# Attention and a gated FFN on one core: the first block's FFN in later slots, and four more score tiles taken transposed

## The chip, the cores and the metric

The kernel runs on one core of a Trainium2 chip. Its engines are TensorE (PE in the profile, its weight loads PEld), VectorE (DVE), ScalarE (ACT), GpSimd (POOL), and SyncE (SP), which here only issues DMAs. The metric is the time of one execution on the device in microseconds (us). The kernel before takes 1466.86 us (median of three runs, 1466.7 to 1467.34).

## The reference

For each of 4 batches, with S = 3136 rows, 256 columns and keys of width 64:

```python
scores = (1 / S) * z @ z.T              # S x S: keys and queries are the same z
x = u * (np.maximum(scores, 0) ** 2 @ v)  # attention without a softmax, gated by u
h = np.maximum(x @ w_in, 0)             # 256 -> 1024
conv = conv_w[0] * h[t - 1] + conv_w[1] * h[t] + conv_w[2] * h[t + 1]   # along the rows
out = (h * sigmoid(conv)) @ w_out       # 1024 -> 256
```

The score matrix of a batch is symmetric: the tile of keys j under queries q is the transpose of the tile of keys q under queries j.

## The kernel before

**Tiles.** The queries of a batch are cut into 6 blocks of 512 and a remainder of 64, the keys into 25 tiles of 128 (the last holds 64 rows, twice). All products are made of float32 values that are split into a high and a low part, so that one logical matmul is two or three on TensorE: 2 for a score tile (lines 409 and 410), 6 for a tile's share of the attention (line 535: three for each half of the 256 columns), 6 for one FFN input tile of 128 columns (`ffn_in`, lines 705 to 708), 6 for one FFN output share (`ffn_out`, lines 780 to 782, three for each half).

**Slots.** The whole program is written out by hand as 600 slots, one for each key tile of each of the 24 blocks; every engine executes its instructions in the order in which the slots name them. In slot k TensorE does the attention of tile k (`attend`) and the scores of tile k + 4 (`scores`); the other engines prepare tiles k + 2 and k + 3. A score tile s in PSUM becomes t = relu(s) on ScalarE (line 489, three buffers `t`), is squared on VectorE (line 504; on ScalarE for the tiles in `SQ`), is cast to the high part `ah` on ScalarE (line 513) and subtracted to the low part `al` on VectorE (line 171). `al` is the last reader of the score bank. There are two banks `s`; for tiles below `K_O` the odd ones use `ph` (block 0) or `o0`/`o1` instead, so that four are in turn.

**Transposed tiles.** Where the symmetry allows, a block doesn't score a tile but takes what an earlier block has: there GpSimd copies relu(s) as two halves of 16 bits to a buffer `pl` (`part`, line 439, three buffers), SP writes it to DRAM (`spill`, line 452), and ten slots before its use SP reads it back with a transposing DMA (`fetch`). ScalarE then squares it, and for even slots squares it a second time into `ah`; VectorE only makes `al` (in odd slots also the cast). `Q0` says how many query blocks of batch 0 score the four tiles of block 0's columns for themselves; from block `Q0` on these come transposed, and block 0 writes them out (`entries`, `own`, `part`).

**FFN.** When a block's attention is done, `gate_x` takes it from the two `av` banks and multiplies by u in the first slot of the next block; `split_x` makes the two parts `xh` and `xl`. Then the eight FFN tiles f follow in slots given by `FS`, counted from the block's first slot: `ffn_in` into one of two banks `ph`, a relu and a first tap on ScalarE, two convolution steps on VectorE (line 749), a sigmoid, a gate product (line 763, four slots after `ffn_in`, the last use of the bank), the split, and `ffn_out` ten and eleven slots after `ffn_in`, into `o0` and `o1`. `evac` and `store` write the block's result 12 and 14 slots after the last tile's slot. The banks `ph` serve two other things once a block: the ring score (line 377, freed by a relu on ScalarE, line 383) three slots before the block begins, and from block 2 on an early score of the last key tile (line 546, freed by a copy, line 551), in most blocks in slot 6.

**Weights.** The weights come as 64-bit floats and are turned into two float32 parts on the chip, in 16 pieces (8 of `w_in`, 8 of `w_out`, in the order of need) that begin in the slots `WS` and are loaded four slots earlier. A piece takes four instructions on VectorE (lines 316, 320, 328, 333), two and a cast on ScalarE (lines 325, 326, 174), a product and a subtraction on GpSimd (lines 338 and 171). Its intermediate values lie in a PSUM bank (`wp` in the trace) for pieces that begin before slot `W_P` and those in `W_B`, in SBUF (`wr`) for the others.

**What else block 0 holds.** In the first 25 slots GpSimd and ScalarE also split the keys (`zl`, `zh`) and the values (`vv`).

Of the kernel before, what the change touches and what calls it, by code (L numbers as in the profile page):

```python
# [30 lines left out]
DG = [1, 8, 15, 22]  # L31


K_O = 35
Q0 = 3
C0 = [0, 1, 2, 3, 16, 17, 22, 23, 4, 5, 18, 19, 8, 9, 20, 21, 6, 7, 10, 11, 14, 15, 12, 13, 24]

FS = [2, 5, 8, 11, 15, 18, 21, 24]  # L40
RELU, TAP, ST1, ST2, SIG, GATE, GHI, OUT0, OUT1 = 1, 2, 2, 3, 4, 4, 5, 10, 11
EVAC = 12
UL = 18
XS = 1

C_GATE, C_ST1, C_ST2, C_G, C_SIG, C_HI = 0, 2, 2, 2, 1, 3
C_RELU, C_TAP, C_XS, C_EV, C_V = 3, 1, 3, 3, 5
# [2 lines left out]
WARM = 7  # L50
VO = 4
Z1 = -3
WS = [2, 6, 8, 12, 16, 19, 21, 25, 27, 33, 36, 38, 40, 41, 46, 52]
WST = [0, 1, 1, 2, 3]
W_E = ["GGGGGGGGGGGGGGGG", "AAAAAAAAAAAAAAAA"]
W_C = 7
W_A = [9, 14]
W_B = [6, 7]
SQ = [26, 46]
W_P = 22  # L60

# [18 lines left out]
def kernel(  # L80
# [21 lines left out]
    NJ = (S + P - 1) // P  # L102
# [5 lines left out]
    FC = DFF // P  # L108
# [12 lines left out]
    def own(b, q):  # L121
        return CB if b == 0 and q < Q0 else 0

# [273 lines left out]
    def scores(k):  # L397
# [3 lines left out]

        if k < K_O and k % 2:
            tag, n = ("ph", 2) if k < NJ else (f"o{k // 2 % 2}", 1)
# [23 lines left out]
    def part(k):  # L427
# [3 lines left out]
        if x is not None and x < CB - 1:  # L431
            src = rl[k][:, (x + 1) * P : (x + 2) * P if x else NB]
        elif x is None and not (tr or r < (Q0 if b == q == 0 else q + 1) or (r == QB and q >= RB)):
            src = rl[k]
# [384 lines left out]
    V, A, G = nc.vector, nc.scalar, nc.gpsimd  # L819
# [4 lines left out]
    PRE, MID, VEC, POST, PE0, PE1 = range(6)  # L824

    def at(slot, cls, fn, *args):
        ev[slot][cls].append((fn, args))
# [3 lines left out]
    for q in zs[2:]:  # L831
        s = min(C0.index(j) for j in range(q * CB, min(q * CB + CB, NJ))) - LA - 3
# [11 lines left out]
    for b in range(1, B):  # L844
        k0 = (b * QB - 1) * NJ
        for q in range(QB + 1):
            s = k0 - (QB - 2 - q) * NJ + (12 if q % 2 == 0 else 4)
            if q == QB - 2:
                s = k0 + 6
            elif q == QB - 1:  # L850
                s = k0 + NJ + 6
            elif q == QB:
                s = k0 + 9
            if b == 1 and q < 2:
                s = (Q0 - QB) * NJ + NJ + k0 + 4 + 8 * q
            at(s - 4, POST, load_z, b, q)
            at(s, POST, prep_z, q)
        last = {j: i for i, (j, _) in enumerate(ent[b - 1][QB - 1])}
        for j in range(0, NJ, 2):
            s = k0 + max(last[j] + 2, last.get(j + 1, 0) + 2, V0 + V1 * j // NJ)  # L860
            if j == NJ - 1:
                s = k0 + V0 - 2
# [5 lines left out]
    for blk in range(1, NBLK):  # L868
        s = blk * NJ + E3
# [4 lines left out]
    for blk in range(PK, NBLK):  # L874
        s = blk * NJ + (R_E if blk % QB == RB else E24[blk % QB])
# [6 lines left out]
    for b in range(B):  # L882
# [9 lines left out]
        for i in range(n + 1):  # L892
            s = k5 + (R_J + 2 * i + R_L * (i == n - 1) // 2 if i < n else R_D + 1) + 1
# [14 lines left out]
    def prep_w_at(n, what, f, i, s):  # L908
        if not wps and W_P:
            wps["w"] = ps.tile([P, 2, D], F32, tag="o1", name="wp")  # L910
        bank = wps["w"] if s < W_P else None
        if i in W_B and not n:
            bank = ps.tile([P, 512], F32, tag="ph", name="wp", bufs=2).rearrange("p (a n) -> p a n", a=2)
        prep_w(n, what, f, *(E[x[i]] for x in W_E), bank, nc.gpsimd if i in W_A else None)

    need = [(NJ + FS[f], "in", f) for f in range(FC)] + [(NJ + FS[f] + OUT0, "out", f) for f in range(FC)]
    for i, (_, what, f) in enumerate(sorted(need)):
        s = WS[i]
        at(s - 4, POST, load_w, what, f)
# [2 lines left out]
    for n in range(4):  # L922
        at(W_C + n, POST, prep_conv, n)
    for blk in range(NBLK):
        at(blk * NJ + UL, POST, load_u, blk)

    def before_end(slot, *args):
        if slot < NS:
            at(slot, *args)

    for blk in range(NBLK - 1):
        k0 = (blk + 1) * NJ
        at(k0, C_GATE, gate_x, blk, G)
        at(k0 + XS, C_XS, split_x, blk, (V, G))
        for f in range(FC):
            s = k0 + FS[f]
            if s == NS - 1:
                break
            at(s, POST, ffn_halo, blk, f)
            at(s, PE1, ffn_in, blk, f)  # L940
            at(s + RELU, C_RELU, ffn_relu, blk, f)
            at(s + RELU, C_RELU, ffn_keep, blk, f)
            at(s + TAP, C_TAP, ffn_tap, blk, f)
            at(s + ST1, C_ST1, ffn_conv, blk, f, 1)
            at(s + ST2, C_ST2, ffn_conv, blk, f, 2)
            before_end(s + SIG, C_SIG, ffn_sig, blk, f)
            before_end(s + GATE, C_G, ffn_gate, blk, f, G)
            before_end(s + GHI, C_HI, ffn_hi, blk, f, A)
            before_end(s + GHI, PE1, ffn_lo, blk, f, G)
            before_end(s + OUT0, PE0, ffn_out, blk, f, 0)  # L950
            before_end(s + OUT1, PE0, ffn_out, blk, f, 1)
        if blk < NBLK - 2:
            at(s + EVAC, C_EV, evac, blk)
            at(s + EVAC + 2, POST, store, blk)
# [97 lines left out]
    def run(fns):  # L1052
        for fn, args in fns:
            fn(*args)

    with tc.manual_schedule():
# [15 lines left out]
        for k in range(-LA, NS):  # L1072
            e = ev[k]
            run(e[PRE])
            early = k + LT < K_O
            if early and 0 <= k + LT:
# [81 lines left out]
```

## Time and profile before

| | |
|---|---|
| median of three runs | 1466.86 us |
| profiled execution | 1467.12 us |
| its span, first to last instruction | 1465.3 us |
| busy PE, PEld | 1451.6 us, 1260.7 us |
| busy DVE, ACT, POOL | 1143.4, 1178.5, 864.0 us |
| matmuls | 6781 |
| granted TensorE clock, mean | 1.000 |

A busy time is the time in which at least one instruction of the engine is recorded. Records of neighbouring instructions overlap, those of matmuls most: one of 512 columns is recorded with 0.38 us and the next begins 0.22 us later. So the share of busy time says little of how full TensorE is, and counts of matmuls in a stretch say more. Block 0 runs from 8.4 to 55 us, block 1 to about 120 us, block 2 to 180 us.

### The profile page before, as it was taken

What the parts mean: (1) busy time and instruction counts of PE and PEld (TensorE: products, weight loads), DVE (VectorE), ACT (ScalarE), POOL (GpSimd) and SP (SyncE); (2) the same over time, 40 slices, a digit from 0 to 9 for tenths busy, and PEclk for the clock granted to TensorE, in tenths of its full rate; (3) what the DMA queues carried; (4) which work ended last, traced back from release to release, by engine and by line L of the source; (5) the groups of instructions that cost most, each with busy time, mean ns of one, the idle gap of its engine ahead of it and who ended that gap; (6) DMA issues with size and microseconds to landing.
All of it is one profiled execution on the core that took longest, in us unless ns stands there. A gap on an engine that the chain in (4) does not pass through costs nothing.

```text
span 1465.3 us, 22715 instructions
## 1 busy us (share of the span) xinstructions
PE 1451.6 (99%) x6781; PEld 1260.7 (86%) x6781; DVE 1143.4 (78%) x1776; ACT 1178.5 (80%) x2246; POOL 864.0 (59%) x1218
## 2 busy tenths in 40 slices
PE   9999999999999999999999999999999999999998
PEld 7778888888888888888888888888888888888887
DVE  8998777768787777767777877876778777787677
ACT  8878887878877877878888788787887777878767
POOL 7875656447866654545776654554586654554433
PEclk9999999999999999999999999999999999999999
DMA  6544666865445556678444555586644446567621
GB/s 198 164 132 104 153 142 156 169 150 138 147 134 142 135 132 157 138 149 178 133 149 132 138 140 134 140 172 138 157 149 137 132 122 150 129 132 168 133 63 37
DMA packets 432380, 205.24 MB, mean 140 GB/s; under 512 B 330753, under 2 KB 411905, under 8 KB 432257
## 3 DMA queue, kind: packets, MB, share of 16 engines
q1 hardware_dynamic: 431584, 203.40, 56.9%
q8 instruction: 53, 0.87, 0.3%
q14 instruction: 71, 0.57, 0.1%
q10 hardware_dynamic: 672, 0.40, 0.1%
HBM read 36.59 MB, written 86.90 MB: 84 GB/s over the span
## 4 chain that ended last, share of the span: by engine, by line
PE 87%; POOL 4%; ACT 3%; DVE 3%; issue 2%; DMA 0%; SPq 0%; ACTq 0%; POOLq 0%; DVEq 0%
PE av L535 46%; PE ph L708 5%; PE o L780 5%; PE o L782 5%; PE ph L705 5%; PE o L781 5%; PE ph L706 5%; PE s L409 4%; PE s L410 4%; PE av L617 1%; DVE ph L749 1%; POOL vv L171 1%; POOL pl L439 1%; ACT ph L744 1%; DVE al L171 1%
## 5 line engine op out<-in xcount | busy, mean ns | idle before, releaser
L535 PE MATMUL av<-ah,vv 128*128 128x512 f32 x2400 | 708.7, 379 | 1.4 <-ACT ah L513 0.7
L171 DVE TENSOR_TENSOR al<-s,ah 128x512 fp32r<-128x512 f32 x576 | 397.5, 690 | 225.4 <-PE av L535 116.8
L535 PEld LDWEIGHTS av<-ah,vv 128*128 128x128 f32 x2400 | 449.5, 189 | 64.9 <-ACT ah L513 1.1
L535 PE MATMUL av<-al,vv 128*128 128x512 f32 x1152 | 437.0, 379 | 0.4
L171 POOL TENSOR_TENSOR gl<-hb,gh 128x512 fp32r<-128x512 f32 x192 | 245.3, 1277 | 157.1 <-ACT gh L174 149.3
L749 DVE SCALAR_TENSOR_TENSOR ph<-hb,cw,ph 128x512 f32<-128x512 f32 x384 | 286.8, 747 | 9.4 <-ACT ph L744 9.0
L439 POOL COPY pl<-t 128x1024 uint16<-128x1024 uint16 (+1 forms) x257 | 260.9, 1017 | 2.2 <-DMA dq<-pl 1.1
L535 PEld LDWEIGHTS av<-al,vv 128*128 128x128 f32 x1152 | 217.7, 189 | 32.6 <-DVE al L171 1.8
L504 DVE TENSOR_TENSOR s<-s,t 128x512 f32<-128x512 f32 x275 | 191.8, 697 | 61.5 <-ACT t L489 60.8
L489 ACT ACTIVATE t<-s 128x512 f32<-128x512 f32 x277 | 166.1, 599 | 64.1 <-PE s L410 60.0
L513 ACT CAST ah<-s 128x512 fp32r<-128x512 f32 x277 | 163.3, 590 | 59.8 <-DVE s L504 59.5
L756 ACT ACTIVATE ph<-ph 128x512 f32<-128x512 f32 (+1 forms) x200 | 115.4, 577 | 78.1 <-DVE ph L749 74.7
L739 POOL COPY halo<-hb 128x2 f32<-128x2 f32 x160 | 31.1, 194 | 240.6 <-ACT hb L734 232.2
L484 ACT ACTIVATE s<-tp 128x512 f32<-128x512 f32 x278 | 165.3, 596 | 4.9 <-DMA tp<-dd 3.0
L705 PE MATMUL ph<-xh,wih 128*128 128x512 f32 x384 | 145.8, 380 | 1.1 <-DVE hb L763 1.1
L780 PE MATMUL o<-gh,wol 128*128 128x512 f32 x384 | 145.9, 380 | 0.0
L782 PE MATMUL o<-gl,woh 128*128 128x512 f32 x384 | 145.5, 379 | 0.0
L706 PE MATMUL ph<-xh,wil 128*128 128x512 f32 x384 | 145.5, 379 | 0.0
L781 PE MATMUL o<-gh,woh 128*128 128x512 f32 x384 | 145.5, 379 | 0.0
L744 ACT ACTIVATE ph<-hb,cw 128x512 f32<-128x512 f32 x192 | 133.7, 696 | 6.2 <-POOL halo L739 0.4
L763 DVE TENSOR_TENSOR hb<-ph,hb 128x512 f32<-128x512 f32 x192 | 131.8, 686 | 5.1 <-ACT ph L756 0.7
L734 ACT ACTIVATE hb<-ph 128x512 f32<-128x512 f32 x192 | 114.2, 595 | 17.7 <-PE ph L708 16.3
(138 smaller groups left out, 2091.3 us busy)
## 6 DMA issues: line engine op xcount, KB each, us to landing
dq<-pl SPq DMA_DIRECT2D x232, 256.0 KB, 2.7
st<-in_v_dram SPq DMA_DIRECT2D x48, 256.0 KB, 3.1
ut<-in_u_dram SPq DMA_DIRECT2D x24, 512.0 KB, 4.1
out_dram<-ob SPq DMA_DIRECT2D x19, 512.0 KB, 3.8
st<-in_z_dram SPq DMA_DIRECT2D x24, 256.0 KB, 3.2
sh<-sc SPq DMA_DIRECT2D x44, 128.0 KB, 2.4
dd<-pl SPq DMA_DIRECT2D x69, 64.0 KB, 2.2
dd<-pl SPq DMA_DIRECT2D x23, 192.0 KB, 2.4
```

What stands on the lines that cost most here:

```text
L171: eng.tensor_tensor(out=out, in0=a, in1=b.bitcast(F32), op=ALU.subtract)
L439: nc.gpsimd.tensor_copy(pl[k], src.bitcast(U16).rearrange("p (n h) -> p h n", h=2))
L484: nc.scalar.activation(sc[k][:, :NB], tp[k], AF.Square, scale=SC1**-0.5)
L489: nc.scalar.activation(rl[k], sc[k][:, :NB], AF.Relu, scale=SC1)
L504: nc.vector.tensor_tensor(out=s, in0=s, in1=rl[k], op=ALU.mult)
L535: nc.tensor.matmul(o, lhsT=w[:, j, d], rhs=pairs(r), start=first and i == 0, stop=last and i == len(ops) - 1)
L705: nc.tensor.matmul(o, lhsT=wih[:, dc, w], rhs=pairs(xh[blk][:, dc]), start=(dc == 0), stop=False)
L706: nc.tensor.matmul(o, lhsT=wil[:, dc, w], rhs=pairs(xh[blk][:, dc]), start=False, stop=False)
L749: nc.vector.scalar_tensor_tensor(out=c, in0=hb[blk, f][:, k : e + k], scalar=cw[:, f, k : k + 1], in1=c, op0=ALU.mult, op1=ALU.add,)
L780: nc.tensor.matmul(o, lhsT=wol[:, f, d], rhs=pairs(h), start=(f == 0), stop=False)
L781: nc.tensor.matmul(o, lhsT=woh[:, f, d], rhs=pairs(h), start=False, stop=False)
L782: nc.tensor.matmul(o, lhsT=woh[:, f, d], rhs=pairs(l), start=False, stop=(f == FC - 1))
```

## The change

Block 0's FFN begins in slot 32 and no longer in slot 27: a block's FFN lags by `max(0, 5 - block)` slots, and while it does its eight tiles come every third slot (`FSL`), so that the lag is gone with block 5. `split_x` moves with it; `gate_x` doesn't. The loads of u for blocks 2 and 3 are two slots and one slot later. The pieces of the weights begin in later slots, the last in 57 instead of 52, and piece 8 too uses a PSUM bank. `K_O` goes from 35 to 40: five more slots in which odd score tiles use the banks `o0` and `o1` and a relu is issued ahead of the cast. `Q0` goes from 3 to 2: block 2 takes its tiles of keys 0 to 3 transposed, and block 0 writes out tiles 8 to 11, which it didn't before.

```diff
-K_O = 35
-Q0 = 3
+K_O = 40
+Q0 = 2
 FS = [2, 5, 8, 11, 15, 18, 21, 24]
+FSL = [2, 5, 8, 11, 14, 17, 20, 23]
+LAG = 5
-WS = [2, 6, 8, 12, 16, 19, 21, 25, 27, 33, 36, 38, 40, 41, 46, 52]
+WS = [2, 6, 10, 13, 17, 20, 24, 28, 32, 36, 39, 43, 46, 49, 53, 57]
-W_B = [6, 7]
+W_B = [6, 7, 8]
...
-    need = [(NJ + FS[f], "in", f) for f in range(FC)] + [(NJ + FS[f] + OUT0, "out", f) for f in range(FC)]
+    def lag(blk):
+        return max(0, LAG - blk)
+
+    def ffn_slots(blk):
+        x = lag(blk)
+        return [(blk + 1) * NJ + x + s for s in (FSL if x else FS)]
+
+    need = [(s + o, w, f) for w, o in (("in", 0), ("out", OUT0)) for f, s in enumerate(ffn_slots(0))]
...
-        at(blk * NJ + UL, POST, load_u, blk)
+        at(blk * NJ + max(UL, lag(blk - 2) + 15 if blk > 1 else 0), POST, load_u, blk)
...
-        at(k0 + XS, C_XS, split_x, blk, (V, G))
-        for f in range(FC):
-            s = k0 + FS[f]
+        at(k0 + XS + lag(blk), C_XS, split_x, blk, (V, G))
+        for f, s in enumerate(ffn_slots(blk)):
```

## Rows read from the trace of the kernel before

**Rows 1.** The page, part 4: the chain that ended last, by engine.

```profile
PE 87%; POOL 4%; ACT 3%; DVE 3%; issue 2%; DMA 0%; SPq 0%; ACTq 0%; POOLq 0%; DVEq 0%
```

**Rows 2.** Busy time by stretch: length, each engine's busy time (instructions), clock, DMA share, GB/s.

```profile
40.00:60.00 20.00, 19.04 (x84) 14.94 (x83) 19.20 (x38) 17.39 (x39) 16.39 (x22) 1.00 0.61 180
60.00:80.00 20.00, 19.28 (x86) 15.52 (x85) 18.88 (x33) 17.16 (x36) 13.50 (x21) 1.00 0.39 109
80.00:100.00 20.00, 17.94 (x81) 14.50 (x81) 19.33 (x34) 16.50 (x35) 14.91 (x20) 1.00 0.45 130
100.00:120.00 20.00, 19.54 (x90) 16.40 (x89) 18.19 (x29) 16.46 (x34) 17.04 (x25) 1.00 0.50 147
...
140.00:200.00 60.00, 60.00 (x283) 52.62 (x282) 46.90 (x71) 48.61 (x91) 35.44 (x49) 1.00 0.65 146
```

**Rows 3.** Waits of PEld, 8 to 120 us: us in total, times, longest.

```profile
PEld s L409 <- DVE al L171: 5.3, 9, 2.0
```

**Rows 4.** Waits of ACT, 8 to 120 us.

```profile
ACT t L489 <- POOL pl L439: 1.3, 2, 1.1
```

**Rows 5.** DMA issues, 0 to 60 us: count, size, median us to landing.

```profile
dq<-pl SPq DMA_DIRECT2D x12, 256.0 KB, 3.2
```

**Rows 6.** POOL groups, 28.8 to 51.02 us: count, busy us, mean ns, idle before them.

```profile
L439 POOL COPY pl<-t 128x1024 uint16<-128x1024 uint16 x7 | 7.2, 1041 | 0.0
...
L338 POOL TENSOR_TENSOR wr<-wr 128x256 f32<-128x256 f32 x4 | 2.9, 735 | 1.1 <-DVE wr L333 1.1
L171 POOL TENSOR_TENSOR wil<-wr,wih 128x256 fp32r<-128x256 f32 x4 | 2.9, 733 | 0.0
```

**Rows 7.** DVE groups by form, 8 to 120 us.

```profile
L749 DVE SCALAR_TENSOR_TENSOR ph<-hb,cw,ph 128x512 f32<-128x512 f32 x14 | 10.4, 745 | 0.0
L328 DVE SCALAR_TENSOR_TENSOR wr<-wr 128x256 uint32<-128x256 uint32 x7 | 4.9, 697 | 0.0
...
L316 DVE TENSOR_SCALAR wr<-wr 128x256 uint32<-128x256 uint32 x7 | 4.0, 573 | 0.0
...
L328 DVE SCALAR_TENSOR_TENSOR wr<-wr,wp 128x256 uint32<-128x256 uint32 x8 | 3.7, 466 | 0.0
L320 DVE TENSOR_SCALAR wr<-wr 128x256 uint32<-128x256 uint32 x7 | 3.6, 520 | 0.0
L333 DVE SCALAR_TENSOR_TENSOR wr<-wr 128x256 f32<-128x256 uint32 x5 | 3.0, 605 | 0.0
```

**Rows 8.** DVE in order of time, 92 to 99 us: start, us, line.

```profile
92.77 0.68 DVE L171 TENSOR_TENSOR al<-s,ah 128x512 fp32r<-128x512 f32 x1
93.37 0.69 DVE L504 TENSOR_TENSOR s<-s,t 128x512 f32<-128x512 f32 x1
93.97 0.68 DVE L763 TENSOR_TENSOR hb<-ph,hb 128x512 f32<-128x512 f32 x1
```

**Rows 9.** All engines in order of time, 48 to 56 us: the end of block 0.

```profile
49.96 1.04 POOL L439 COPY pl<-t 128x1024 uint16<-128x1024 uint16 x1
...
51.29 0.59 ACT L489 ACTIVATE t<-s 128x512 f32<-128x512 f32 x1
...
54.14 0.44 ACT L174 CAST woh<-wr 128x256 fp32r<-128x256 f32 x1
...
55.15 1.24 PE L535 MATMUL av<-ah,vv 128*128 128x512 f32 x3 [0.60 <-ACT x L667]
```

**Rows 10.** The same, 110 to 116 and 136 to 138 us: users of `ph`.

```profile
110.08 0.38 PE L705 MATMUL ph<-xh,wih 128*128 128x512 f32 x1
...
112.44 0.68 DVE L763 TENSOR_TENSOR hb<-ph,hb 128x512 f32<-128x512 f32 x1
...
113.97 0.60 PE L535 MATMUL av<-ah,vv 128*128 128x512 f32 x2
...
114.84 0.40 ACT L383 ACTIVATE dg<-ph 128x256 f32<-128x256 f32 x1
...
137.16 0.59 ACT L551 COPY sc<-ph 128x512 f32<-128x512 f32 x1
137.33 0.59 PE L535 MATMUL av<-ah,vv 128*128 128x512 f32 x2
```

## The prediction, before the kernel was run

> **What bounds the kernel now.** I read the page first: of the chain that ended last TensorE holds 87% and no other engine over 4% [rows 1]; the span is 1465.3 us. Over most of the run TensorE sets the time, and only a change in its work, or a stall of TensorE, moves the end. Next the busy times by stretch [rows 2]. The busy share is of little use (a matmul's recorded time overlaps the next), the count of matmuls is: 283 in the 60 us from 140 on, so a matmul of full width takes 0.212 us and 20 us hold 94.3. From 40 to 120 us they hold 84, 86, 81 and 90. The shortfall is 10.3 matmuls (2.2 us) from 40 to 60, and 8.3, 13.3 and 4.3 (25.9, or 5.5 us) from 60 to 120. From 140 on it holds its rate. So about 8 us can be had from stalls, all in block 0's last slots and in the two stages after. The reader is to see that VectorE is busy 18.2 to 19.3 us of every 20 there, GpSimd 13.5 to 17.0. Third the waits: TensorE waits nine times (5.3 us in its weight loads) for VectorE's `al`, the last reader of a score bank [rows 3]; ScalarE waits for GpSimd's copy of a score tile to `pl` in 1.3 us [rows 4]. The granted clock is 1.00 in all these stretches.
>
> I use slots: one key tile of one query block, 25 a block. A slot without FFN is 8 matmuls, 1.7 us.
>
> **The change, part by part.**
>
> *Eight matmuls go.* In block 2 four tiles are no longer scored but come transposed: 4 x 2 x 0.212 = 1.7 us. Block 2 lies in the stretch at full rate [rows 2], so I take all of it; bounded by 1.7 and, if that stretch waits for something else then, 0. Their VectorE squares (0.69 us each [rows 8]) go too; ScalarE squares twice where it had a relu and a copy. Four transposes of 256 KB join SP's queue, ten slots ahead. Four transposed tiles of block 2 were there before, in the stretch from 140 on, and lost nothing [rows 2]; the DMA share there is 0.65. So I put the new four at nothing; were that cover gone, a late tile would hold TensorE for about one landing, 3.2 us [rows 5].
>
> *Four GpSimd copies, and four spills, come into block 0.* With `Q0` 2 the tiles 8 to 11 are written out as well: parts at positions 4 to 7, 10 to 15 and 18 to 23, where 12, 13, 18 and 19 had none. GpSimd is full there: from 28.8 to 51.0 us its only gap is 1.1 us, before a weight piece's product on line 338 [rows 6]. To the copy for tile 23, which ends at 51.0 us [rows 9], the new order adds 4 x 1.04 = 4.2 us, loses one weight step (0.73 us) through the later pieces, and can use the gap: 4.2 - 0.7 - 1.1 = 2.4. Who waits: there are three `t` buffers, so ScalarE's relu three tiles on waits for the copy, and behind that relu, in order, stand the casts to `ah` and block 0's scaled evacuation on line 667, for which TensorE waits at 55.15 us [rows 9]. The relu began 0.3 us after the copy's end, and a weight cast in between (0.44 us) moves later: 2.4 - 0.7 = 1.7 us lost. Bounds: 0, if the order of the buffers leaves slack, and 2.4 + 1.1 = 3.5, if the gap stays. I take 1.7, since GpSimd has no other gap. The spills queue on SP behind GpSimd's copies; with three `pl` buffers and a landing of 3.2 us [rows 5] against copies 1.7 us apart or more they just fit.
>
> *The FFN begins five slots later and the pieces are spread.* This takes work away from VectorE where it was late. Its instructions begin 0.09 us before their forerunner's record ends (they start at 92.77, 93.37 and 93.97, with records of 0.68 to 0.69) [rows 8]. Slots 36 to 42 before (79 to 100 us): 6 squares and 7 `al` of 0.69 (9.0 us), 4 convolution steps of 0.75 (3.0), 2 gate products of 0.68 (1.4), 4 weight pieces (begun at 36, 38, 40 and 41) of 0.57 + 0.52 + 0.70 + 0.61 = 2.4 (9.6) [rows 7, 8]: 22.9 us in 35 records, so 35 x 0.09 less, 19.8 us. TensorE has 14 score, 42 attention and 24 FFN matmuls: 80, or 17.0 us. The difference, 2.8 us, is what the stretch from 80 to 100 lost (13.3 matmuls). After: the same 13 and 4, 3 products, 2 pieces: 18.8 in 28 records, 16.3; TensorE 14 + 42 + 15 = 71, 15.1 us. Left: 1.2 us, and in front of the heavier of the two pieces stands a slot with an FFN input, which gives VectorE some lead; I keep 0.6. Slots 27 to 35 hold 33 VectorE instructions of 21.7 us (18.7 with the overlap) against 90 matmuls (19.1), level, so that every burst showed; after, three convolution steps and two products are gone and one `xl` has come: 15.8 against 84 matmuls (17.8), 2 us of room. Slots 43 to 57 are below as well (29 instructions, 16.6 us, against 17.3 in the first seven). I keep 1.2 of the 5.5 us in all, 0.6 of it in slots 46 to 56: 4.3 us gained. Bounds: 5.5 (all goes) and 0 (the stalls only move). Moved with it, at no cost: `split_x`, five slots later, with its two ScalarE casts and one subtraction each on VectorE and GpSimd (GpSimd is by then free of block 0's copies); the loads of u for blocks 2 and 3, two slots and one slot later on SP, still five and six slots ahead of their use; the loads of the pieces, four slots ahead of each. `K_O` 40 leaves the scores of tiles 35 to 39 in four banks instead of two, until the FFN needs them: that loosens the wait of rows 3 for five slots, and is in the 4.3.
>
> Piece 8 goes from SBUF to a PSUM bank: line 328 takes 697 ns on SBUF and 466 on the bank [rows 7], so some 0.5 us of VectorE, in the sum above by being no burst. [...]
>
> *A new wait.* `ph` has two banks. An FFN tile holds one from its slot s to the gate product at s + 4, so with a pitch of three a third user fits only when it comes one or two slots after an FFN input. Before, all do. With the lag, the ring score of block 2 is in slot 47 = 25 + 5 + 17, the early score of block 2 in slot 56 = 50 + 4 + 2, the ring score of block 5 in slot 122 = 100 + 2 + 20: each in the very slot of an FFN input, and ahead of it in TensorE's order. So the input must wait for the third bank: for the ring's relu, the early copy, or the gate product, and everything of TensorE stands behind it. From the rows of before [rows 10]: the next matmul after the ring of block 2 could begin at 113.97 and the ring's relu ends at 115.24, 1.3 us, and I take the same for block 5's; after the early score it is 137.33 and 137.75, 0.4. That makes 3.0; 0.8 of it lies over what would be lost in slots 46 to 56 anyway (the 0.6 above, and the 0.2 of the ring's own matmuls), 2.2 remain. If it is the gate product: TensorE could begin at 110.08 and the product ends at 113.12, 3.0, less the ring's two half matmuls, 2.8 each, 8.4 in all. I take 2.2, because the relu and the copy read banks filled just before and stand near the front of ScalarE's queue, and the allocation takes the bank that comes free first; the other end stays in the range.
>
> Sum: -1.7 + 1.7 - 4.3 + 2.2 = -2.1 us. The profiled execution took 1467.12 us (span 1465.3 and 1.8 around it), so 1465.0; it is 0.26 above the median of 1466.86, which gives 1464.8.
>
> **The rivals.**
>
> *All stalls go (A).* GpSimd's lateness finds slack and the waits for `ph` fall where VectorE needs the time: -1.7 + 0 - 5.5 + 0.7 + 0.8 = -5.7, 1461.2. For it: after block 0 GpSimd is busy 13.5 of 20 us [rows 2] and catches up. Against: no gap in rows 6.
>
> *The gate product releases the bank (B), slower.* Place: slots 47, 56 and 122; price 8.4 instead of 2.2: -1.7 + 1.7 - 4.3 + 8.4 = +4.1, 1471.0. It decides from the point where the three waits together pass 4.3 us, 1.4 each. For it: the product comes before the relu in the written order of the slot. Against: it stands behind a subtraction and a square on VectorE, the ring's relu behind less.
>
> *The stalls move (C).* VectorE stays the bound to slot 60, with the same loss some slots later, and the waits for `ph` lie inside it: -1.7 + 1.7 + 0 = 0.0, 1466.9. For it: from slot 22 to 46 VectorE loses nearly as much work (one piece, three convolution steps, a product, some 5 us) as TensorE (21 matmuls, 4.5 us). Against: it is the bunch of four pieces that showed, not the total.
>
> **How the numbers follow.** Forecast 0.46, A 0.22, B 0.20, C 0.12. 0.2% is 2.9 us, about what a measurement can tell from no change. Of the forecast's own range (1462.8 to 1466.8) a quarter lies beyond that: 0.12 faster, 0.34 within. A is faster (0.22). B is slower by 0.18, within by 0.02. C is within, 0.11, and 0.01 slower. Faster 0.34, within 0.47, slower 0.19. The range takes in most of A and B: 1460.4 to 1470.2.
>
> **What would show it.** Right: matmuls from 60 to 120 us at 90 or more in each 20; the copy for tile 23 ending near 53 us, and block 1's first attention matmul near 56.9 instead of 55.15; three gaps of TensorE before line 705 of 0.4 to 1.3 us near 115, 138 and 290. Wrong: gaps of 2 us or more there, released by line 763 (B); no lateness at 55 (A); `al` still holding line 409 for microseconds past 100 us (C). A stall in block 2 that ends with a transpose would show a cost that I put at nothing.

## The result, and the profile after

The changed kernel takes 1486.57 us (median of five runs, 1484.98 to 1492.69), the kernel before in the same set 1466.88: 19.7 us more, a ratio of 1.0141 with a 95% interval of 1.0118 to 1.0165. The forecast was 1464.8, the range 1460.4 to 1470.2. The time goes with TensorE's granted clock: 1484.98 and 1485.49 us at a mean of 0.998, 1492.69 at 0.994. The profile is of this last run, the longest (span 1490.9 us, where before had 1465.3).

The chain that ended last, by engine [rows 1 before]: TensorE has lost 5 points and GpSimd 2; ScalarE has 3 more, VectorE 2.

```profile
PE 82%; ACT 6%; DVE 5%; issue 3%; POOL 2%; DMA 1%; SPq 1%; ACTq 0%; POOLq 0%; DVEq 0%
```

The busy times by stretch, with the columns of [rows 2]:

```profile
40.00:60.00 20.00, 16.94 (x70) 11.58 (x68) 16.05 (x30) 15.76 (x35) 19.23 (x27) 1.00 0.71 216
60.00:80.00 20.00, 20.00 (x85) 16.98 (x86) 17.11 (x31) 14.29 (x31) 10.15 (x14) 0.91 0.33 98
80.00:100.00 20.00, 15.74 (x71) 12.69 (x70) 18.51 (x30) 15.78 (x34) 14.82 (x22) 1.00 0.52 156
100.00:120.00 20.00, 17.31 (x71) 14.12 (x70) 16.58 (x27) 14.09 (x29) 11.83 (x17) 0.89 0.60 170
120.00:140.00 20.00, 18.71 (x81) 15.54 (x80) 15.12 (x24) 15.21 (x31) 12.27 (x17) 0.94 0.37 99
140.00:200.00 60.00, 55.59 (x246) 47.67 (x246) 42.12 (x64) 45.07 (x86) 34.95 (x50) 0.94 0.49 119
```

Two things are to be seen. From 80 to 120 us TensorE has 142 matmuls where it had 171. And the granted clock, 1.00 in every stretch before, is 0.89 to 0.94 in four of these six. From about 325 us on hardly more is lost.

What TensorE waited for from 8 to 330 us (us in total, times, longest): the score banks still wait for `al` (line 411, 409 before), and a wait for `ph` at the FFN input (line 707, 705 before), which the list of before doesn't have in this stretch, has four releasers.

```profile
PE s L411 <- DVE al L173: 7.6, 5, 2.2
PE ph L707 <- DVE hb L765: 3.2, 1, 3.2
PE ph L707 <- ACT dg L385: 2.0, 2, 1.4
PE av L537 <- ACT x L669: 1.8, 2, 1.5
PE ph L707 <- ACT rj L599: 1.4, 1, 1.4
...
PE ph L707 <- ACT sc L553: 0.3, 1, 0.3
```

Before, the same stretch has for the score banks:

```profile
PE s L409 <- DVE al L171: 2.5, 3, 1.6
```

The changed kernel in order of time, matmuls with the idle time before them in brackets:

```profile
59.02 0.70 PE L537 MATMUL av<-ah,vv 128*128 128x512 f32 x2 [1.53 <-ACT x L669]
...
88.83 0.50 PE L411 MATMUL s<-zq,zh 128*128 128x512 f32 x1 [1.97 <-DVE al L173]
...
115.60 0.76 PE L411 MATMUL s<-zq,zh 128*128 128x512 f32 x1 [2.15 <-DVE al L173]
...
117.75 0.79 PE L707 MATMUL ph<-xh,wih 128*128 128x512 f32 x1 [0.54 <-ACT dg L385]
118.34 0.63 PE L708 MATMUL ph<-xh,wil 128*128 128x512 f32 x1
118.77 0.63 PE L707 MATMUL ph<-xh,wih 128*128 128x512 f32 x1
...
147.30 0.79 PE L707 MATMUL ph<-xh,wih 128*128 128x512 f32 x1 [3.19 <-DVE hb L765]
...
288.05 0.48 PE L707 MATMUL ph<-xh,wih 128*128 128x512 f32 x1 [1.43 <-ACT rj L599]
```

The matmuls of 512 columns behind 117.75 and 147.30 start 0.43 us apart, with records of 0.63 us, where others start 0.22 apart: that is the granted clock at 0.5, 1.2 GHz instead of 2.4. It holds at 60.9 to 64.3, 115.5 to 122.3 and 146.2 to 153.0 us, 17 us in all. TensorE works in some 15.3 of them (in the rest it waits), and at 1.00 would have needed half: about 7.6 us lost. The trace of before has no such stretch before its last matmuls.

At the end of block 0 the sixteenth copy to `pl`, that for tile 23 (the twelfth before, ending at 51.00 [rows 9]), ends at 54.20. The copy for tile 25, the first of block 1, ends at 58.34, and for it block 0's scaled evacuation waits: its result `x` lies in one of the three buffers `t` too, the one that tile 25 had.

```profile
53.17 1.03 POOL L441 COPY pl<-t 128x1024 uint16<-128x1024 uint16 x1
...
56.62 0.74 POOL L173 TENSOR_TENSOR wil<-wr,wih 128x256 fp32r<-128x256 f32 x1 [0.77 <-ACT wih L176]
57.30 1.04 POOL L441 COPY pl<-t 128x1024 uint16<-128x1024 uint16 x1
...
58.38 0.60 ACT L669 ACTIVATE x<-av 128x512 f32<-128x512 f32 x1 [0.85 <-POOL pl L441]
```

The same copy and the evacuation before:

```profile
53.43 1.04 POOL L439 COPY pl<-t 128x1024 uint16<-128x1024 uint16 x1
...
54.50 0.60 ACT L667 ACTIVATE x<-av 128x512 f32<-128x512 f32 x1
```

And some of VectorE's weight steps take over a microsecond. VectorE and GpSimd in order of time:

```profile
92.32 2.11 POOL L441 COPY pl<-t 128x1024 uint16<-128x1024 uint16 x2
92.39 1.13 DVE L318 TENSOR_SCALAR wr<-wr 128x256 uint32<-128x256 uint32 x1
93.45 1.13 DVE L322 TENSOR_SCALAR wr<-wr 128x256 uint32<-128x256 uint32 x1
94.50 0.68 DVE L173 TENSOR_TENSOR al<-s,ah 128x512 fp32r<-128x512 f32 x1
```

Each step runs about as long as a GpSimd copy beside it (two copies in 2.11 us). By groups from 56 to 165 us, the form on SBUF has a mean of 798 ns (573 before in 8 to 120 us, line 316 of [rows 7]), the same step into a PSUM bank 481:

```profile
L318 DVE TENSOR_SCALAR wr<-wr 128x256 uint32<-128x256 uint32 x7 | 5.6, 798 | 0.0
...
L318 DVE TENSOR_SCALAR wp<-wr 128x256 uint32<-128x256 uint32 x3 | 1.4, 481 | 0.0
```

### The profile page after: what moved, and what is told of

Its sections match the earlier page's. It is cut to its first block, busy times and chain, and to the rows that moved or that the text cites. A ratio compares the mean times of both kernels' runs of the same rounds, so it can differ in the third digit from the quotient of the medians.

```text
span 1490.9 us, 22692 instructions
## 1 busy us (share of the span) xinstructions
PE 1460.4 (98%) x6773; PEld 1264.2 (85%) x6773; DVE 1144.9 (77%) x1773; ACT 1180.0 (79%) x2245; POOL 866.9 (58%) x1222
## 4 chain that ended last, share of the span: by engine, by line
PE 82%; ACT 6%; DVE 5%; issue 3%; POOL 2%; DMA 1%; SPq 1%; ACTq 0%; POOLq 0%; DVEq 0%
PE av L537 42%; PE ph L707 5%; PE ph L710 5%; PE ph L708 5%; PE o L784 5%; PE o L782 5%; PE o L783 5%; PE s L411 4%; PE s L412 4%; PE av L619 2%; DVE ph L751 1%; DVE al L173 1%; ACT t L491 1%; DMA dq<-pl 1%; ACT s L486 1%
## 5 line engine op out<-in xcount | busy, mean ns | idle before, releaser
L441 POOL COPY pl<-t 128x1024 uint16<-128x1024 uint16 (+1 forms) x261 | 264.9, 1017 | 2.5 <-DMA dq<-pl 0.8
```

The lines of the kernel that those rows point to most:

```text
L441: nc.gpsimd.tensor_copy(pl[k], src.bitcast(U16).rearrange("p (n h) -> p h n", h=2))
```

## The experiments

Differences are between medians of one set of runs ("over before"), with the ratio of the means and its 95% interval.

### The clashes for `ph`, and `Q0`

The slots show four clashes, not three: the scores of batch 0's remainder (line 592) lie in slot 113, an FFN input's slot as well (`R_D`, their slot counted from block 5's first, is -12). e1 moves the four users two slots ahead:

```diff
-        s = blk * NJ + E3
+        s = blk * NJ + E3 - (2 if blk in (2, 5) else 0)
...
-        s = blk * NJ + (R_E if blk % QB == RB else E24[blk % QB])
+        s = blk * NJ + (R_E if blk % QB == RB else E24[blk % QB]) - (2 if blk == 2 else 0)
...
+        R_D = -14 if b == 0 else -12
```

> The changed kernel with the four users that meet an FFN input in one slot (ring scores of blocks 2 and 5, early score of block 2, batch 0's remainder scores) moved two slots ahead, so that each comes one slot after an FFN input. Theory D (the double-booked banks, and the lower TensorE clock after the long waits, make most of the loss): the waits of TensorE for ph fall from 8.4 us to under 1.5, the half-clock stretches at 115 and 146 us go, and the time falls from 1486.6 to 1472 to 1477. Rival V (VectorE and GpSimd are late from slot 36 on, and the banks only show it): the waits move to al, at least 4 us of the 8.4 come back there, and the time stays at 1481 to 1486.

1479.7 us, 11.6 over before (1.0081, 1.0069 to 1.0094): 8.1 of the 19.7 us gone. Taken over 1466.88 us, theory D's range is 5.1 to 10.1 us and V's 14.1 to 19.1: the result lies between them, nearer to D. The wait for `ph` is down to one, and `al` did not take it over:

```profile
PE s L411 <- DVE al L173: 6.3, 4, 2.1
...
PE ph L707 <- ACT sc L553: 0.3, 1, 0.3
```

The stretch at half clock behind slot 47 is gone; one of 3.4 us comes at 147.8, and that at the start of block 1 stays. The next two set `Q0` alone.

```diff
-Q0 = 2
+Q0 = 3
```

> The changed kernel with Q0 back at 3: the lag, the spread pieces and K_O 40 alone; the eight matmuls of block 2 and no copies of tiles 8 to 11 in block 0. Theory D: block 1's first attention matmul is back at 55.2 us, the half-clock stretch at 61 us goes, the work is 1.7 us more, the clashes stay: 1481 to 1485. Rival V (the four GpSimd copies of block 0 push GpSimd's and VectorE's queues back into the stretch of the pieces, and the clash waits come from that): 1470 to 1477, with waits for ph under 4 us.

1485.8 us, 17.8 over before (1.0120, 1.0107 to 1.0134): 1.9 less than the changed kernel, just outside D's range as it is written, and far from V's. The waits for `ph` are as long as with `Q0` 2 (3.2 + 2.2 + 1.4 us), so they don't come from block 0's copies. The stretch at half clock at 61 us is gone. Block 1 begins at 56.46 us, not at 55.2 as D had it: 1.3 us of its lateness come without the four copies.

e3 is the kernel before with `Q0` at 2:

> The kernel before with Q0 at 2 alone: no lag, old slots of the pieces. Terms of the prediction: -1.7 for the matmuls and +1.7 for block 0's copies: 1466.9. Theory D: TensorE loses 3.2 us at the end of block 0 as in the changed kernel (its first attention matmul of block 1 near 59) and a half-clock stretch follows: 1468.5 to 1472. Rival (VectorE is late anyway after slot 27, so that the lateness of block 0 vanishes in it): 1465 to 1467.5.

1470.85 us, 2.8 over before (1.0020, 1.0011 to 1.0029), as D has it. Block 1 begins at 58.44 us, and in the profiled run the clock is at 0.5 from 59.7 to 63.1.

e4 is the lag as it was meant: e1 with `Q0` at 3.

> Q0 at 3 and the four users two slots ahead: the lag, the spread pieces and K_O 40 as they were meant. Theory D: 1467 to 1472, with waits for al left in slots 36 to 50 of 2 to 5 us, and no half-clock stretch inside the span. By the prediction's own term (4.3 us of VectorE stalls gone): 1462.5. Rival V: 1476 or more.

1478.4 us, 10.3 over before (1.0071, 1.0057 to 1.0085). The clashes cost 7.5 us here (17.8 less 10.3), as much as with `Q0` 2, but the rest is far above D, in V's range (1476 or more), and farther still above the prediction's 1462.5. One stretch at half clock is left, at 57.8 us, where D had none. What is left is in the lag, the pieces and `K_O`.

Did `Q0` cost through something else? With it the keys of batch 1 are prepared 25 slots earlier, which the prediction didn't mention. f4 is e3 with the old slots for them:

```diff
-                s = (Q0 - QB) * NJ + NJ + k0 + 4 + 8 * q
+                s = (3 - QB) * NJ + NJ + k0 + 4 + 8 * q
```

> The kernel before with Q0 at 2 and the first two parts of batch 1's keys prepared in slots 79 and 87 as before (with Q0 at 2 they come in slots 54 and 62). If that move, which the prediction didn't see, is what costs in slots 48 to 55 (1.2 us): 1 us or more under Q0 alone (which took 2.8 us over before), so 1.0 to 1.9 over. If block 0's four copies are all: 2.3 to 3.3 over.

1470.83 us, 2.6 over before (1.0018, 1.0009 to 1.0027): it is not that. What is left are block 0's four copies with their spills, and four more transposes. Nor is it the clock: f4's trace has no stretch at half clock before its last matmuls, and of e3's eleven runs five have a mean of 1.000, too high for a stretch of 3.4 us, and take no less (1470.93 us in the median, the six others 1470.84).

### The lag, the pieces and `K_O` one by one

e5 is e4 with `K_O` back at 35.

> The lag without clashes and with Q0 at 3 (1478.4 us, 10.3 over the kernel before), with K_O back at 35. Theory K (the four score banks in turn up to tile 39 only put VectorE's debt off, and at slot 38, where two banks are left, it is paid at once: the gap of 2.0 us there): the gap at slot 38 shrinks by 1 us or more, others of the same sum come in slots 32 to 37, and the time stays at 1477 to 1480. Rival (the new order of relu and cast in slots 32 to 36 costs by itself): 1473 to 1476.

1481.9 us, 14.6 over before (1.0096, 1.0082 to 1.0110). Both expectations fail: `K_O` 40 gains 4.3 us in this kernel (14.6 less 10.3, from two sets). The gap in slot 38 shrinks by 0.9 us, but one of 1.6 comes in slot 32, and, in the profiled run, a second stretch at half clock.

e7 takes the pieces back too, and is the lag alone:

```diff
-WS = [2, 6, 10, 13, 17, 20, 24, 28, 32, 36, 39, 43, 46, 49, 53, 57]
+WS = [2, 6, 8, 12, 16, 19, 21, 25, 27, 33, 36, 38, 40, 41, 46, 52]
...
-W_B = [6, 7, 8]
+W_B = [6, 7]
```

> As e5, with the pieces of the weights in their old slots and piece 8 in SBUF: the lag of the FFN alone. Theory P (the spread pieces cost: in their new slots VectorE's SBUF steps meet busy GpSimd stretches and stand in front of al): 1468 to 1472, with gaps for al in slots 45 to 60 under 1 us in all. Rival L (the lag itself costs, since VectorE's FFN steps of block 0 now fall in slots 46 to 60, where block 1's own come too): 1474 to 1478, with the gaps of slots 49 to 59 (5.5 us) still there.

1476.7 us, 9.4 over before (1.0063, 1.0050 to 1.0075): in L's range, so the lag itself costs most. But L has the place wrong: of its gaps in slots 49 to 59 little is left, and the loss has moved to slots 28 to 47. P has a share too: the spread pieces, piece 8 in a bank among them, cost 5.2 us (14.6 less 9.4). They shorten slots 36 to 46 by 2.3 us, which is what the change was after, but block 1 begins 1.2 us later (56.60 against 55.37), slots 25 to 27, at half clock in e5, take 1.6 us more, and slots 50 to 59 5.0. From 80 to 100 us in e7:

```profile
80.00:100.00 20.00, 15.16 (x66) 11.56 (x65) 19.46 (x32) 14.84 (x32) 14.74 (x20) 1.00 0.42 129
```

VectorE is busy 19.5 of 20 us, as before (19.33 [rows 2]), and TensorE has 66 matmuls where it had 81. Slots 28 to 46 last 51.6 us with 194 matmuls, before 50.0 with 210: taking 16 matmuls out (18 of the FFN, while two of the moved ring score came in; 16 x 0.212 = 3.4 us) shortened nothing, and they come back in later slots at full price (slots 60 to 89 have 9 more and last 1.9 us longer). Nor did VectorE's own time fall there: its records add up to 51.7 us in 75 instructions, before 52.2 in 79. Its 24 weight steps, in the same slots as before, take 15.9 us instead of 13.8. There is a further loss of some 3 us in slots 100 to 124 in every kernel that lags by five, the clashes not counted: 0.7 of it is a wait of the moved remainder scores and 0.9 one of the remainder's attention. That FFN steps of blocks 2 and 3 now stand ahead of other work there is my reading, not shown.

g3 is the lag alone with `LAG` at 2 (only the two users of block 2 moved):

> The lag alone (e7: 9.4 us over the kernel before) with LAG 2 instead of 5: blocks 0 and 1 lag by two slots and one, the two users that would meet an FFN input are moved. Theory M (FFN matmuls moved out of slots 27 to 45, where VectorE and GpSimd set the pace, come back later at full price): the cost goes with the lag, 2 to 5 us over before. Rival (single collisions at the ends of blocks 1 to 4 and in slots 49 to 59 make it): under 1.5 over. The prediction's own reading (less FFN in those slots removes the stalls): 1 us or more under before.

1472.2 us, 4.7 over before (1.0036, 1.0024 to 1.0049): in M's range, half of what five slots cost, and the loss in slots 100 to 124 is gone. The prediction's reading falls with it.

e9 spreads pieces without a lag, in the kernel before:

```diff
-WS = [2, 6, 8, 12, 16, 19, 21, 25, 27, 33, 36, 38, 40, 41, 46, 52]
+WS = [2, 6, 8, 12, 16, 19, 21, 25, 27, 33, 36, 39, 42, 45, 48, 52]
```

> The kernel before with the pieces 11 to 14 in slots 39, 42, 45 and 48 instead of 38, 40, 41 and 46: no lag. By the prediction's own reading (the bunch of four pieces in slots 36 to 42 makes the gap of 1.65 us in slot 39): 1465.5 to 1467 against 1468.1, the gap gone. Rival C of the prediction (VectorE stays the bound, the gap moves some slots on): 1467.5 to 1468.5. Theory S (what counts is which GpSimd instruction the steps meet): anything between 1466 and 1470, with single steps of 0.9 us and more in new places.

1468.9 us, 1.6 over before (1.0010, 1.0001 to 1.0019). The gap of slot 39 is gone, and gaps of 1.21, 0.76 and 0.60 us come in slots 46, 49 and 55; ahead of the first stand two weight steps of 0.98 and 1.11 us. That is above the ranges of the prediction's own reading and of rival C, and in that of theory S. The bunch made the gap of slot 39, but spreading it gains nothing.

### VectorE's steps beside GpSimd

m1 runs five of VectorE's forms eight times each, with GpSimd idle, then copying, then subtracting, back to back. Shortened, the forms are:

```python
V.tensor_scalar(out=expo, in0=hi, ...)              # L134: SBUF to SBUF
V.tensor_scalar(out=half, in0=hi, ...)              # L137: SBUF to PSUM
V.scalar_tensor_tensor(out=outa, in0=hi, in1=mant, ...)  # L140: two SBUF inputs
V.scalar_tensor_tensor(out=outb, in0=hi, in1=bank, ...)  # L143: one input in PSUM
V.tensor_tensor(out=sz, in0=bank, in1=sx, ...)           # L146: one input in PSUM
```

> No part of the computation: eight each of VectorE's shift (SBUF to SBUF, and SBUF to PSUM), its join of two SBUF inputs, the same with one input in PSUM, and a subtraction with one input in PSUM; three times: GpSimd idle, GpSimd copying 16-bit halves back to back, GpSimd subtracting back to back. Theory S: the two that touch only SBUF take 0.28 to 0.6 us alone and 0.9 us or more beside either GpSimd instruction; those with a PSUM operand keep their times within 10%. [...] Rival (the steps are slow for another reason, such as DMAs): no form changes by over 10%.

Groups of VectorE from 9 to 27 us (GpSimd idle), 28.7 to 60 (its copies of 1.04 to 1.11 us) and 73.6 to 106 us (its subtractions of 1.26 to 1.33):

```profile
L137 DVE TENSOR_SCALAR half<-raw 128x256 uint32<-128x256 uint32 x8 | 3.4, 427 | 0.2
L140 DVE SCALAR_TENSOR_TENSOR outa<-raw,mant 128x256 uint32<-128x256 uint32 x8 | 3.4, 424 | 0.2
...
L134 DVE TENSOR_SCALAR expo<-raw 128x256 uint32<-128x256 uint32 x8 | 2.3, 293 | 0.2
...
L140 DVE SCALAR_TENSOR_TENSOR outa<-raw,mant 128x256 uint32<-128x256 uint32 x8 | 9.0, 1130 | 0.2
L134 DVE TENSOR_SCALAR expo<-raw 128x256 uint32<-128x256 uint32 x8 | 7.8, 973 | 0.2
...
L137 DVE TENSOR_SCALAR half<-raw 128x256 uint32<-128x256 uint32 x8 | 3.4, 426 | 0.2
...
L140 DVE SCALAR_TENSOR_TENSOR outa<-raw,mant 128x256 uint32<-128x256 uint32 x8 | 10.3, 1283 | 0.2
L134 DVE TENSOR_SCALAR expo<-raw 128x256 uint32<-128x256 uint32 x8 | 9.4, 1172 | 0.2
```

Theory S holds: both forms that touch only SBUF, the shift with a single input too, become about as long as GpSimd's instruction; the form into PSUM doesn't change, nor do L143 (420 and 419 ns) and L146 (690). The Trainium skill (SBUF — State Buffer, Who interferes with whom) has both cases: two SBUF inputs beside a GpSimd instruction that reads SBUF, and a tensor_scalar in a mode that uses both port pairs. The trace agrees with the waiting (1130 and 973 ns beside the copies); the mode that the shift runs in no run shows.

e8 is e5 with pieces 9 and 10 in a bank, and piece 9's low part back on VectorE:

```diff
-W_A = [9, 14]
+W_A = [14]
...
+        if i in (9, 10) and not n:
+            bank = ps.tile([P, 2, D], F32, tag="o1", name="wp")
```

> As e5, with the intermediate values of pieces 9 and 10 in a PSUM bank (o1) and piece 9's low part on VectorE. Theory S (steps with SBUF in and out wait for GpSimd: 0.9 to 1.4 us instead of 0.3 to 0.35): the steps of these two pieces take 0.4 to 0.5 us, the gaps of slots 38 to 41 (4.3 us) fall under 2, and the time is 2 to 3 us under e5. Rival (VectorE's count of instructions there is too high, whatever they take): within 1 us of e5.

1477.8 us, 10.5 over before (1.0071, 1.0057 to 1.0084), 4.1 under e5. The gaps of slots 38 to 41 fall from 3.4 to 1.2 us, slots 36 to 42 from 20.7 to 18.7 us, and in the profiled run e5's two stretches at half clock (3.4 us each) don't come; 1.0 us more is lost in slots 47 to 55. The 4.1 us are more than theory S had (2 to 3). At the same mean clock, 0.999, e5's one run and e8's three lie 2.0 to 2.4 us apart.

f3 takes one such step away in e4, where the trace shows in slot 59:

```profile
145.25 1.44 POOL L564 TENSOR_TENSOR sh<-sc,sh 128x512 f32<-128x512 f32 x1
145.49 1.48 DVE L335 SCALAR_TENSOR_TENSOR wr<-wr 128x256 f32<-128x256 uint32 x1
146.89 0.68 DVE L173 TENSOR_TENSOR al<-s,ah 128x512 fp32r<-128x512 f32 x1
...
147.62 0.48 PE L411 MATMUL s<-zq,zh 128*128 128x512 f32 x1 [2.79 <-DVE al L173]
```

```diff
-W_A = [9, 14]
+W_A = [9, 14, 15]
```

> The lag without clashes and with Q0 at 3 (e4: 1478.4 us, 10.3 over the kernel before), with the low part of piece 15 made on ScalarE and GpSimd, so that VectorE's step of 1.48 us beside GpSimd's early sum in slot 59 isn't there. Theory S: the gap of slot 59 (2.7 us) shrinks to under 1.7 us, and the time to 8.0 to 9.3 us over before. Rival (VectorE is full there whatever the step): the gap moves, 9.8 us or more over before.

1476.6 us, 8.3 over before (1.0056, 1.0042 to 1.0069), 2.0 under e4. The gap is 0.36 us and did not move:

```profile
145.14 0.48 PE L411 MATMUL s<-zq,zh 128*128 128x512 f32 x1 [0.36 <-DVE al L173]
```

### The clock

g5 adds four stalls to the kernel before, where TensorE hardly ever waits. Shortened:

```python
nc.tensor.matmul(p, lhsT=zp, rhs=zh[:, :512], start=True, stop=True)
nc.scalar.copy(y, p[:, :RQ])
for i in range(n):   # n = 2, 5, 8, 11
    nc.gpsimd.tensor_tensor(out=x, in0=y.bitcast(F32), in1=y.bitcast(F32), op=ALU.add)
    nc.gpsimd.tensor_tensor(out=y, in0=x, in1=x, op=ALU.subtract)
...
nc.tensor.matmul(q[:, :RQ], lhsT=zp, rhs=y, start=True, stop=True)
```

> The kernel before with four stalls of TensorE added in blocks 7, 9, 13 and 15, where it otherwise never waits: a matmul, a copy on ScalarE, 4, 10, 16 and 22 small GpSimd instructions in a chain, and a matmul that needs them. Theory H (the wait itself brings the clock down): behind the longer of the stalls the granted clock is 0.5 for 3.4 us or more, behind the shortest it stays 1.0, and the time rises by the stalls and 1.7 us or more for each stretch at 0.5. Rival (the clock fell in the changed kernel for what the other engines did): it stays 1.0, and the time rises by the stalls alone.

1497.5 us, 30.0 over before (1.0205, 1.0191 to 1.0219). The last matmul of each stall:

```profile
452.49 0.30 PE L878 MATMUL ph<-sy,zp 128*128 128x64 f32 x1 [1.79 <-POOL sy L876]
...
576.47 0.42 PE L878 MATMUL ph<-sy,zp 128*128 128x64 f32 x1 [4.02 <-POOL sy L876]
...
823.33 0.42 PE L878 MATMUL ph<-sy,zp 128*128 128x64 f32 x1 [6.25 <-POOL sy L876]
...
952.80 0.42 PE L878 MATMUL ph<-sy,zp 128*128 128x64 f32 x1 [8.47 <-POOL sy L876]
```

and the stretches around the falls of the clock:

```profile
453.00:457.00 4.00, 4.00 (x13) 3.20 (x12) 2.79 (x5) 1.14 (x3) 2.67 (x4) 0.57 0.36 77
...
576.00:580.00 4.00, 3.53 (x10) 2.92 (x11) 0.69 (x1) 0.00 (x0) 2.67 (x5) 0.57 0.03 6
...
822.00:829.00 7.00, 5.67 (x14) 4.58 (x15) 1.38 (x2) 0.00 (x0) 4.26 (x8) 0.51 0.15 33
...
948.00:959.00 11.00, 6.20 (x16) 5.05 (x17) 1.38 (x2) 0.00 (x0) 6.14 (x16) 0.53 0.12 25
```

Theory H holds, and more than it said: the shortest stall too was followed by 3.4 us at half clock. The stalls add up to 20.5 us. Behind them TensorE works at 0.5 for 3.4, 3.2, 5.6 and 5.8 us, 18.0 in all, so 9.0 lost. The two sums make 29.5 of the 30.0 us. The fall does not come at each gap: the lagged kernels have one of some 2 us in slot 38, and of e1, e2, e4 and f3 only f3 shows the fall there. Nor does it cost the same everywhere: f3's run at a mean of 1.000 took 1476.22 us, its two at 0.997 1476.57 and 1476.91, though 0.003 of the span are 4.4 us.

### A version under both

f1 is the kernel before with `K_O` at 40 and nothing else:

> The kernel before with K_O at 40 alone. Theory K2 (four score banks give the chain relu, square, cast, al slack, where two leave none; 3.5 us with the lag): the gaps of slots 32 to 36 (1.1 us) go and 0.5 to 1.5 us are gained: 1465.5 to 1467. Rival (ffn_out needs o0 and o1 in slots 37 and 38, and waits for the score tiles in them): 1468 to 1470.

1466.19 us, 2.1 under before (0.9985, 0.9977 to 0.9994), more than the 0.5 to 1.5 us expected. By the stretches it is gained where [rows 2] had 86 and 81 matmuls:

```profile
60.00:80.00 20.00, 19.51 (x92) 16.61 (x91) 19.05 (x34) 17.60 (x37) 13.83 (x21) 1.00 0.37 109
80.00:100.00 20.00, 18.75 (x84) 15.33 (x84) 18.50 (x35) 16.81 (x36) 16.00 (x21) 1.00 0.52 151
```

Two variants of it, `W_B` with piece 8 and `W_A` with piece 13:

> The kernel before with K_O 40 (2.1 us under it), and piece 8's intermediate values in a PSUM bank. Theory S (steps with a PSUM operand don't wait for GpSimd): its four VectorE steps take 0.4 to 0.5 us each and 0 to 1 us more is gained. Rival (the bank ph is missed by the FFN inputs of slots 27 and 30): 0.5 to 2 us over K_O 40 alone.

> The kernel before with K_O 40, and the low part of piece 13 made on ScalarE and GpSimd: its VectorE step took 1.11 us beside GpSimd at 99 us. Theory S: the gap of slot 46 (0.6 us) or what stands before it shrinks, 0 to 0.8 us under K_O 40 alone. Rival (GpSimd is full there, and its added 0.7 us makes something else late): 0 to 1 us over.

1465.4 us (0.9988, 0.9979 to 0.9997) and 1465.9 us (0.9990, 0.9981 to 0.9999), 2.1 and 1.7 under before: no difference from f1 that can be told. Where nothing lags, single slow steps cost little.

## Why the prediction was wrong

By its own steps, over before: the lag, pieces and `K_O` without clashes +10.3 (forecast -4.3), `Q0` +1.3 on top of that (forecast 0.0), the clashes +8.1 (forecast +2.2). They make the 19.7.

**"The FFN begins five slots later and the pieces are spread. This takes work away from VectorE where it was late."** This step failed, by its sign. It compared VectorE's work with TensorE's as sums over slots and credited the difference. Three things are wrong in it. In slots 28 to 46 VectorE and the order of its steps set the pace, so TensorE's FFN work there was hidden; moved out, it frees nothing and is paid later (e7; g3 agrees). The records of [rows 7] were taken as prices, but a step on SBUF has two: 0.29 or 0.42 us beside an idle GpSimd, over 0.97 beside a busy one (m1), and both the moved pieces (f3, e8) and the unmoved ones beside a moved FFN (e7, 15.9 us in place of 13.8) meet it at other times. And VectorE need not be full to hold `al`: in the changed kernel's slots 36 to 42 its records cover 18.6 of 21.0 us (forecast 16.3); the rest, as I read it, is waiting in the chain of relu, square, cast and `al`, whose slack is the number of score banks. `K_O` 40, which adds such banks and had no term of its own, is the part that gains: 4.3 us with the lag and 2.1 without.

**"A new wait."** The mechanism was right, the bank that it waits for and its size were not. The forecast took the ring's relu and early copy at 3.0 us; 6.9 were measured (3.2 + 2.0 + 1.4 + 0.3), with the gate product in slot 56 as in rival B and a fourth clash that I had missed in slot 113. The clashes cost 8.1, more than these waits; the lower clock can make the rest (e1's trace has 10.2 us less at half clock). B (1471.0) was nearest of the four cases; it too took the 4.3 us as gained.

**"Four GpSimd copies."** A term mis-sized, by a path that it didn't have. The copy for tile 23 ends at 54.20 us, 3.2 later than before (forecast 2.4), and the relu that waits for it begins at 54.23. But block 1 begins at 59.02, not 56.9, since block 0's evacuation waits for a later copy, that for tile 25: 58.34 in place of 54.47 us, 3.9 late, and block 1 with it. Ahead of this copy GpSimd stands idle for 0.77 us and makes a weight piece's low part. The later pieces, credited here with 0.7 us, cost instead: with `Q0` 3 block 1 begins at 56.46 and 56.60 us with them (e4, e5), at 55.37 without (e7). With `Q0` alone (e3) 2.8 us are lost; if the eight matmuls gave their 1.7, which no run measures by itself, the copies cost 4.5 in place of 1.7.

**"Eight matmuls go"** held: the profile after has 6773 matmuls, 8 fewer, and no wait of TensorE for the new transposes shows. Rival C had the mechanism of e9 and nearly that of e7: what was taken off the bunch came back some slots later. It had the size too small.

**The clock** stood in no step. That [rows 2] had 1.00 everywhere was read as a constant; it went with TensorE never waiting long. In the profiled run the work at half clock is up to 7.6 of the 25.6 us of added span. The median run had a mean of 0.997, which leaves room for some 4.5 of its 19.7.

What stays open: why one gap brings the clock down and another of the same length doesn't; how the 9.4 us of the lag alone divide between the hidden FFN work, VectorE's longer weight steps and the ends of the blocks; and whether the lag costs or the new pitch of the tiles, since `FSL` comes with the lag in every run.

## What to carry to other kernels

Work of the bounding engine that lies in a stretch where another engine sets the pace was free here; before moving such work out, ask where it will be paid. Give the price of an instruction with what runs beside it, and when two patterns of slots are shifted against each other, list every user of a shared bank or buffer by slot, the rare ones too. A stall of TensorE can cost more than its length, so even waits of 2 us deserve a term for the clock.

## What the runs showed of the hardware

- Two VectorE forms whose operands all lie in SBUF (32-bit, 256 columns) take about as long as the GpSimd instruction beside them: the shift with one input 293 ns alone, 973 beside copies of 1.04 to 1.11 us, 1172 beside subtractions of 1.26 to 1.33; the join of two inputs 424, 1130 and 1283. With one operand in PSUM, the output or an input, they keep their 419 to 427 ns (m1).
- Behind a TensorE stall of 1.79 us the granted clock was 0.5 (1.2 GHz) for 3.4 us, behind one of 8.47 us for 5.8 us more, though TensorE was working all the while; each fall then cost 1.6 to 2.9 us on top of the wait (g5). In e3 and f3, whose traces show the falls in block 1, runs with a mean clock of 1.000 were faster by nothing and by 0.3 to 0.7 us.
